# Weights cast by GpSimd's transfers, w_out centred and scaled in one operation, w in pairs of units, and a new order of work

**Chip, cores, metric.** One core of a Trainium2 chip. The metric is the device time of one execution in microseconds (us); every kernel was run several times on the chip that ran the kernel before in the same session. "Fast" and "slow" are states of an execution: slow is over 1.5% above the fastest of the same kernel.

## The reference

A linear attention (RWKV-6) over 4 sequences of 768 tokens with 8 heads of 48, then a feed-forward layer on 3072 tokens of width 384:

```python
state = w_t * state + k_t v_t^T                 # per head
y_t   = r_t (state + (u * k_t) v_t^T)
h     = y @ w_in                                # 384 x 1024
solu  = h * softmax(h)
out   = (solu - mean) / sqrt(var + 1e-6) * g_ln @ w_out     # 1024 x 384
```

All inputs are float32: r, k, v, w are 4 x 8 x 768 x 48 each, w_in and w_out 1.57 MB each.

## The kernel before

The tokens are cut into 24 units (six chunks of 128 tokens by four sequences). Each unit goes through some thirty stages, and a list of words, `ORDER`, fixes the order in which all engines get their work: `ldk3` loads k of unit 3, `lw3` takes the log of its w, `kp3` scales k and r of unit 3, `kt3` transposes them, `H0` is the first hidden product, `e0` and `he0` its exponential and product, `Oa0` its first output product. Each engine keeps that order, so a word that waits holds back every later word of its engine. A letter at the end of a word names the engine (a ScalarE, v VectorE, g GpSimd).

The inputs, in rows of 192 bytes, and both weights are asked for by SyncE, in one queue:

```python
sp.dma_start(out=L[name], in_=src[b, :, c * C:(c + 1) * C, :].rearrange("h t d -> t h d"))
...
def load_w_in(j):
    sp.dma_start(out=win_f[:, j, :], in_=win_v[:, j, :])
def load_w_out(half):
    part = slice(half * KF // 2, (half + 1) * KF // 2)
    sp.dma_start(out=wout_f[:, part, :], in_=wout_v[:, part, :])
```

w_in is cast on ScalarE (`win`). From w_out comes w2, whose rows are scaled by g_ln and centred: eight gains (`gw`), a mean product (`mean`), eight additions on GpSimd (`wt`):

```python
def setup_w_in(j, engine):
    copy(engine, win_sb[:, j, :], win_f[:, j, :])
def setup_gain(f, engine):
    ...
    engine.tensor_scalar(out=gw[:, f, :], in0=wout_f[:, f, :], scalar1=gr[:, f:f + 1], scalar2=None, op0=MULT)
def setup_mean():
    for f in range(KF):
        pe.matmul(m_ps, lhsT=mean_w, rhs=gw[:, f, :], start=(f == 0), stop=(f == KF - 1))
def setup_w2(f, engine):
    engine.tensor_add(out=w2[:, f, :DM], in0=gw[:, f, :], in1=mean_sb)
```

The start of the order, down to the first hidden products (weights are asked for at `ldwin` and `ldwout`):

```python
dm5 dm3 dm18 dm1 ldw0 ldr0 small dm16 dm8 ldk0 lw0 ldw1 ldr1 cum0 exp0 et0 lw1 rows cum1 ldk1 p0g ldw2 kp0 exp1 ubc kt0 p1g kr0v ldr2 M0 ldk2 ldv0 et1
kp1 lw2 m0a q0g kt1 kr1v ldwin2 cum2 q1g sel0 dg0 exp2 M1 dm10 et2 vb0a kp2 m1a ldwin1 ldv1 kt2 win2a dg1 dv0g kr2v win1a vb1a Y0 y0v sel1 ldwin0 M2
win0a dm6 X0 m2v dv1v ldwout0 dm4 p2g Y1 q2g S1 y1v ldwout1 qa2 gw1a gw0a dm2 X1 xT0v xT1v dg2 H0 H1 ldw3 e0 ...
```

The softmax here doesn't subtract the row's maximum and nothing guards it: scores larger than these inputs give would overflow.

Of the kernel before, what the change touches and what calls it, by code (L numbers as in the profile page):

```python
# [14 lines left out]
SQUARE = mybir.ActivationFunctionType.Square  # L15
IDENTITY = mybir.ActivationFunctionType.Identity
# [8 lines left out]
dm5 dm3 dm18 dm1 ldw0 ldr0 small dm16 dm8 ldk0 lw0 ldw1 ldr1 cum0 exp0 et0 lw1 rows cum1 ldk1 p0g ldw2 kp0 exp1 ubc kt0 p1g kr0v ldr2 M0 ldk2 ldv0 et1  # L25
kp1 lw2 m0a q0g kt1 kr1v ldwin2 cum2 q1g sel0 dg0 exp2 M1 dm10 et2 vb0a kp2 m1a ldwin1 ldv1 kt2 win2a dg1 dv0g kr2v win1a vb1a Y0 y0v sel1 ldwin0 M2
win0a dm6 X0 m2v dv1v ldwout0 dm4 p2g Y1 q2g S1 y1v ldwout1 qa2 gw1a gw0a dm2 X1 xT0v xT1v dg2 H0 H1 ldw3 e0 st1 S0 dm13 ldv2 gw4v gw6v gw3g he0 ldk3
gw5a dm12 dm17 ldw4 st0 gw7a ldr3 e1 ldk4 lw3 gw2g mean mean_sb:a vb2g ldw5 dv2g he1 Y2 ldr4 cum3 wt2g y2v exp3 lw4 et3 p3v hq0a wt3g cum4 wt1g X2 dm0
wt0g ldk5 dm9 ldr5 exp4 lw5 ldw6 wt4g kp3 S2 kt3 ldv3 cum5 st2 ldw7 wt7g ldv4 et4 kr3a xT2v wt6g ldr6 Oa0 kp4 p4v exp5 wt5g M3 q3v et5 m3a kt4 kr4v
ldk6 Oa1 kp5 hq1a H2 M4 q4g kt5 Ob0 ldv5 sel3 ldw8 lw6 vb3a e2 dg3 kr5a dv3g m4v sq0a dg4 vb4g dv4g p5g vb5g Ob1 ldr7 M5 lw7 ldk7 Y3x ldv6 he2 m5v qm0  # L30
q5g p6g y3a cum6 X3 xT3v sq1v Y4 qm1 exp6 y4v H3 lv0 lv1 et6 ldr8 X4 hq2v ldk8 kp6 Oa2 dg5 o0a xT4a dv5g p7g sto0 ldw9 S4 e3 S3 st4 st3 q6g H4 Y5 vb6g
q7g ldr9 o1a he3 kt6 lw8 S5 Ob2 e4 ldk9 y5v cum7 ldr10 he4 kr6a st5 X5 hq3a sq2a exp7 M6 Oa4 ldv7 ldk10 ldr11 Oa3 qm2 m6v cum8 ldv8 qa6 et7 xT5a sto1
dg6 ldr12 ldk11 lv2 kp7 qa7 Ob3 dv6g exp8 p8g ldw10 p9v kt7 et8 o2a dg7 sq3g kp8 H5 qm3 q8g hq4a lv3 ldv9 e5 ldw11 Y6x kr7v ldv10 p10g M7 vb7g o3v Ob4
ldw12 kt8 m7v y6a q10g lw9 X6 sq4v he5 cum9 xT6a qm4 ldk12 exp9 kr8a dg8 et9 dv7g Y7 hq5g H6 e6 sto2 kp9 Oa5 ldw13 kt9 y7v lv4 X7 dg10 q9g Ob5 kr9a
he6 vb8g ldv11 ldk13 dv8g ldr13 sq5a o4a M8 ldw14 hq6g m8v S7 M9 qm5 vb10g xT7a p11g ldv12 m9v lv5 Oa6 H7 dg9 st7 lw10 Y8 o5a e7 cum10 vb9g ldw15
exp10 Ob6 y8v he7 sq6g X8 sto3 et10 dv9g S6 kp10 ldk14 xT8a lw12 S8 q11g H8 lw11 lw13 cum11 st8 e8 dv10g st6 Oa7 qm6 kt10 Y9x p12g exp11 hq7v kr10a
lv6 Ob7 y9a he8 M10 et11 S9 ldw16 sto4 o6a ldr14 X9 xT9a kp11 cum12 qa11 Oa8 ldr15 exp12 hq8g m10v p13g ldv13 vb11g ldk15 st9 H9 sq7v et12 qm7 kt11
q12g ldv14 lw14 ldr16 kp12 ldk16 lv7 e9 Y10x q13g sto5 y10a o7v ldk17 kr11v he9 cum13 exp13 ldv15 et13 dg11 kt12 kp13 Ob8 X10 sto6 M11 kr12a sq8g Oa9
qa12 ldk18 dv11g ldr17 dg13 M12 m12v kt13 ldw17 vb12g xT10a qm8 S10 m11a sel11 H10 kr13v M13 lw15 st10 ldv16 hq9a Y11x lv8 p15g e10 y11a m13v vb13g
sto7 o8a Ob9 dg12 p14g ldr18 ldv17 sq9v dv12g p16g X11 ldw18 cum14 xT11a S11 he10 Y12 H11 exp14 S12 qm9 st11 y12v lv9 et14 kp14 q14g dv13g st12 hq10g  # L40
o9a ldv18 e11 Y13 X12 cum15 xT12a ldr19 he11 exp15 kt14 Oa10 y13v sto8 hq11g kr14a vb15a q15g lw16 S13 H12 vb14g et15 ldk19 kp15 e12 dg14 X13 M14 p17g
dv14g kt15 ldw19 m14v xT13a he12 kr15a Ob10 H13 q17g sto9 hq12g sq10a st13 M15 Y14 m15v ldv19 qm10 lv10 vb16g Oa11 e13 lw18 q16g S14 lw17 o10v y14v
cum16 he13 ldw20 exp16 dg15 et16 hq13v Ob11 dv15g X14 kp16 Oa12 p18g sq11a p19g xT14a st14 qm11 lv11 H14 Ob12 o11a e14 cum17 q19g kt16 sq12v ldk20 Y15
sto10 he14 exp17 q18g qm12 Oa13 sto11 kr16a et17 hq14g y15v cum18 kp17 lv12 Ob13 M16 ldr20 ldk21 o12v exp18 dg17 X15 vb17g sq13v kt17 m16a et18 qm13
Oa14 xT15v kp18 kr17v sel16 lv13 H15 o13a lw19 dg16 e15 kt18 M17 dv17g dv16g vb19g ldv20 kr18v m17a lw20 Ob14 Y16 he15 M18 y16v sq14v S16 qm14 dg18
cum19 X16 ldv21 hq15g xT16v m18a exp19 Oa15 H16 ldw21 sel17 S15 dg19 lv14 o14a et19 kp19 Y17 lw21 ldr21 st16 e16 cum20 sel18 vb18g st15 y17v exp20
Ob15 sto12 ldk22 ldr22 X17 sto13 kt19 sq15v ldv22 xT17a he16 dv18g Y18 qm15 kr19a dv19g kp20 p20v y18v hq16g H17 M19 Oa16 lv15 X18 q20g Ob16 m19v o15a
e17 xT18a ldw22 lw22 p22g cum21 sq16v he17 qm16 p21g dg20 ldw23 hq17g ldv23 exp21 Y19 kt20 H18 vb20g ldr23 Oa17 lv16 y19v kp21 q21g kr20v o16a cum22
e18 he18 dv20g kt21 exp22 Ob17 kr21a M20 X19 sq17g S17 qm17 m20a lv17 kp22 qa21 sel20 lw23 S18 xT19v sto14 o17a st17 hq18g M21 Oa18 ldk23 m21v kt22
cum23 H19 sto15 st18 exp23 kr22v vb21a kp23 dg21 dv21g sto16 Y20 Y21 vb22a M22 q22g S19 e19 m22a vb23g y20v X20 p23v st19 he19 q23g Ob18 kt23 xT20a  # L50
sq18v H20 qm18 kr23a sel22 M23 y21v lv18 o18a X21 dg22 hq19v xT21v Oa19 m23a dv22v dg23 sel23 Y22 Ob19 y22v e20 he20 H21 dv23g Y23 sto17 X22 sq19a
Oa20 y23v X23 qm19 lv19 hq20g o19a xT22v e21 xT23v H22 e22 he21 Ob20 sto18 hq21g sq20a qm20 lv20 H23 he22 Oa21 Oa22 sto19 Ob21 e23 hq22g sq21a o20v
qm21 lv21 Ob22 he23 hq23v Oa23 sto20 sq22v sq23a qm22 o21v Ob23 sto21 lv22 qm23 Oc23 o22v sto22 lv23 dm14 oz23v dm15 o23a stz23 dm7 sto23 dm11 dm19
# [25 lines left out]
def kernel(  # L79
# [14 lines left out]
    C = 128  # L94
# [23 lines left out]
    def load(name, src):  # L118
        def stage(i):
            c, b = units[i]  # L120
            L = live[i]
            if name in "kr":

                if "k_and_r" not in L:
                    L["k_and_r"] = io.tile([C, 2, H, 64], F32, tag="kr_in", name="kr_in")
                t = L["k_and_r"][:, "kr".index(name)]
            else:
                t = io.tile([C, H, 64], F32, tag=name + "_in", name=name + "_in")
            L[name] = t[:, :, :D]
            sp.dma_start(out=L[name], in_=src[b, :, c * C:(c + 1) * C, :].rearrange("h t d -> t h d"))  # L130
        return stage
# [4 lines left out]
    win_f = consts.tile([128, KM, DF], F32)  # L136
    win_v = moe_w_in.rearrange("(ko ki) f -> ki ko f", ki=128)
    wout_f = consts.tile([128, KF, DM], F32)
# [6 lines left out]
    def load_w_in(j):  # L145
        sp.dma_start(out=win_f[:, j, :], in_=win_v[:, j, :])

    def load_w_out(half):
        part = slice(half * KF // 2, (half + 1) * KF // 2)
        sp.dma_start(out=wout_f[:, part, :], in_=wout_v[:, part, :])  # L150
# [3 lines left out]
    nc.gpsimd.memset(uti_neg, -1.0)  # L154
    nc.gpsimd.affine_select(out=uti_neg, in_=uti_neg, compare_op=ALU.is_ge, fill=0.0, base=0,
                            pattern=[[1, C]], channel_multiplier=-1)
    uts = consts.tile([C, C], BF16)
    nc.gpsimd.memset(uts, 1.0)
    nc.gpsimd.affine_select(out=uts, in_=uts, compare_op=ALU.is_gt, fill=0.0, base=0,
                            pattern=[[1, C]], channel_multiplier=-1)  # L160
    ident = consts.tile([C, C], BF16)
    make_identity(nc, ident)
# [12 lines left out]
    lw_t = [consts.tile([C, H, 64], BF16, name=f"lw{j}") for j in range(NR)]  # L175
    kp_t = [consts.tile([C, 2, H, 64], BF16, name=f"kp{j}") for j in range(NR)]
    for j in range(NR):
        nc.vector.memset(lw_t[j][:, :, D:], 0.0)
        nc.vector.memset(kp_t[j][:, :, :, D:], 0.0)
# [7 lines left out]
    mean_w = consts.tile([128, 128], BF16)  # L187
    nc.vector.memset(mean_w, -1.0 / DF)
    nc.vector.memset(w2[:, :, DM:], 1.0 / RDF)

    ident_f = consts.tile([KF, KF], F32)
    make_identity(nc, ident_f)
# [4 lines left out]
    gw = consts.tile([128, KF, DM], BF16)  # L197
# [12 lines left out]

    def copy(engine, out, in_):
# [10 lines left out]
    def setup_w_in(j, engine):  # L222
        copy(engine, win_sb[:, j, :], win_f[:, j, :])


    def setup_gain(f, engine):
        if engine is act:
            act.activation(out=gw[:, f, :], in_=wout_f[:, f, :], func=COPY, scale=gr[:, f:f + 1])
        else:
            engine.tensor_scalar(out=gw[:, f, :], in0=wout_f[:, f, :], scalar1=gr[:, f:f + 1], scalar2=None, op0=MULT)  # L230

    def setup_mean():
        m_ps = small.tile([128, DM], F32, tag="s", name="mean_ps")
        for f in range(KF):
            pe.matmul(m_ps, lhsT=mean_w, rhs=gw[:, f, :], start=(f == 0), stop=(f == KF - 1))
        live[0]["mean_ps"] = m_ps

    def setup_mean_copy(engine):
        copy(engine, mean_sb, live[0]["mean_ps"])

    def setup_w2(f, engine):
        engine.tensor_add(out=w2[:, f, :DM], in0=gw[:, f, :], in1=mean_sb)


    def log_w(i):
        L = live[i]
        L["lw"] = lw_t[i % NR]
# [392 lines left out]
```

## Time and profile before

| | first profile (the prediction's) | second look, taken after it |
|---|---|---|
| time of that execution | 156.91 us, slow | 151.97 us (a single execution, so its state is not decided) |
| span | 155.2 us | 150.3 us |
| first hidden product starts | 20.06 us | 20.06 us |
| matmuls from 25 to 30 us | 34 | 45 |
| matmuls from 80 to 120 us | 628 | 694 |

The median was 151.41 us (151.08 to 151.83).

### The profile page before, as it was taken

The numbers are of one execution on the slowest core, as the hardware profiler recorded it, in microseconds if no ns is written. First come the engines' busy times: TensorE is split into PE (matmuls) and PEld (weight loads), VectorE is DVE, ScalarE is ACT, GpSimd is POOL, SyncE is SP. The second block draws the span as 40 slices with busy tenths as digits, with TensorE's granted clock in tenths as the row PEclk, the third lists the DMA queues.
The fourth block names the chain that finished last, engine by engine and source line by source line (L and its number), as shares of the span: only waits on it lengthen the run. The fifth ranks groups of instructions, "written<-read, shape, count | busy, mean of one in ns | idle before, by whom it ended". The sixth has DMA issues, their size and how long they took to land.

```text
span 155.2 us, 5295 instructions
## 1 busy us (share of the span) xinstructions
PE 140.4 (90%) x2156; PEld 109.7 (71%) x2156; DVE 129.4 (83%) x231; ACT 120.2 (77%) x232; POOL 123.1 (79%) x152
## 2 busy tenths in 40 slices
PE   6877897699999899999999799939999999999993
PEld 2344584477786787888788587737888778889771
DVE  7546738899998898999976989999889999998661
ACT  4456767989898979798989698829899888895742
POOL 3375965997999799999947999977799899976800
PEclk9999999999999999999999999999999999999999
DMA  4999997989999999899796999999989311011013
GB/s 95 201 185 301 380 303 152 213 160 190 208 202 184 204 229 187 194 205 233 154 205 157 218 217 200 228 250 180 215 196 211 100 51 55 2 55 55 18 62 127
DMA packets 104970, 27.09 MB, mean 175 GB/s; under 512 B 100329, under 2 KB 104562, under 8 KB 104946
## 3 DMA queue, kind: packets, MB, share of 16 engines
q1 hardware_dynamic: 104946, 26.75, 76.4%
q8 instruction: 17, 0.28, 0.7%
q14 instruction: 7, 0.06, 0.1%
HBM read 22.03 MB, written 4.72 MB: 172 GB/s over the span
## 4 chain that ended last, share of the span: by engine, by line
PE 50%; DMA 14%; DVE 10%; SPq 8%; POOL 8%; ACT 4%; issue 3%; POOLq 0%; DVEq 0%
PE o_ps L71 18%; PE h_ps L71 13%; SPq L71 8%; DMA kr_in<-in_k_dram 8%; DMA wout_f<-in_moe_w_out_dram 6%; POOL w L71 5%; PE kr_ps L71 5%; PE cum_ps L71 3%; PE m_ps L71 3%; PE y_ps L71 3%; PE s_ps L71 3%; DVE hq L71 3%; DVE kp L71 2%; PE x_ps L71 2%; DVE he L71 1%
## 5 line engine op out<-in xcount | busy, mean ns | idle before, releaser
L71 PE MATMUL o_ps<-w,he 128*128 128x385 bf16 (+2 forms) x200 | 42.2, 315 | 0.3 <-ACT sq L71 0.3
L71 PE MATMUL h_ps<-xT,win_sb 128*128 128x128 bf16 x576 | 36.0, 219 | 0.1
L71 PEld LDWEIGHTS <-win_sb 128*128 128x128 bf16 x576 | 32.9, 98 | 0.9 <-issue 0.2
L71 PE MATMUL o_ps<-inv_col,e 128*128 128x1 bf16 x192 | 31.1, 165 | 0.0
L71 DVE TENSOR_TENSOR he<-h_ps,e 128x1024 bf16<-128x1024 f32 x24 | 29.2, 1217 | 2.2 <-ACT e L71 2.2
L71 POOL TENSOR_TENSOR hq<-he 128x1024 bf16<-128x1024 bf16 x14 | 26.5, 1895 | 3.7 <-DVE he L71 2.4
L71 ACT ACTIVATE e<-h_ps 128x1024 bf16<-128x1024 f32 x24 | 24.5, 1021 | 6.2 <-PE h_ps L71 6.1
L71 PEld LDWEIGHTS <-he 128*128 128x128 bf16 x208 | 19.7, 96 | 10.5 <-issue 0.3
L71 ACT ACTIVATE cum_ps<-cum_ps 128x772 f32<-128x772 f32 (+1 forms) x24 | 19.2, 801 | 8.8 <-PE cum_ps L71 7.6
L71 DVE TENSOR_TENSOR kp<-cum_ps,kr_in 128x768 bf16<-128x768 f32 x24 | 22.7, 948 | 0.6 <-DMA kr_in<-in_r_dram 0.5
L71 POOL TENSOR_TENSOR q<-p,u_bc 128x384 bf16<-128x384 bf16 x23 | 22.0, 962 | 0.6 <-DVE p L71 0.5
L71 POOL TENSOR_TENSOR p<-kr_in 128x384 bf16<-128x384 f32 x18 | 17.9, 1001 | 5.4 <-DMA kr_in<-in_k_dram 5.4
L71 PEld LDWEIGHTS <-kp 128*128 128x128 bf16 x272 | 17.6, 102 | 4.4 <-DVE kp L71 2.3
L71 POOL TENSOR_TENSOR dv<-vb,dg 128x384 bf16<-128x384 bf16 x22 | 18.2, 830 | 2.3 <-ACT vb L71 1.5
L71 DVE TENSOR_TENSOR m<-m_ps,uts 128x1024 bf16<-128x1024 f32 x14 | 17.0, 1223 | 3.1 <-PE m_ps L71 3.0
L71 PEld LDWEIGHTS <-e 128*128 128x128 bf16 x192 | 18.3, 96 | 0.1
L71 PE MATMUL kr_ps<-ident,kp 128*128 128x128 bf16 x192 | 15.9, 230 | 1.4 <-DVE kp L71 1.4
L71 PEld LDWEIGHTS <-kr 64*128 64x128 bf16 (+1 forms) x272 | 10.7, 98 | 4.9 <-DVE kr L71 2.2
L71 ACT ACTIVATE lw<-w_in 128x384 bf16<-128x384 f32 x23 | 11.7, 523 | 2.7 <-DMA w_in<-in_w_dram 2.7
L71 ACT COPY kr<-kr_ps 128x1024 bf16<-128x1024 bf16 x13 | 13.2, 1014 | 0.5 <-PE kr_ps L71 0.4
L71 POOL TENSOR_SCALAR_AFFINE_SELECT m<-m 128x1024 bf16<-128x1024 bf16 x10 | 11.0, 1103 | 2.5 <-ACT m L71 2.4
L71 PE MATMUL cum_ps<-lw,uti_neg 128*128 128x384 bf16 x24 | 8.3, 347 | 4.8 <-DVE kp L71 3.3
(93 smaller groups left out, 284.3 us busy)
## 6 DMA issues: line engine op xcount, KB each, us to landing
w_in<-in_w_dram SPq DMA_DIRECT2D x24, 192.0 KB, 4.2
kr_in<-in_r_dram SPq DMA_DIRECT2D x24, 192.0 KB, 3.8
kr_in<-in_k_dram SPq DMA_DIRECT2D x24, 192.0 KB, 3.8
v_in<-in_v_dram SPq DMA_DIRECT2D x24, 192.0 KB, 3.8
out_dram<-o SPq DMA_DIRECT2D x23, 192.0 KB, 3.1
win_f<-in_moe_w_in_dram SPq DMA_DIRECT2D x3, 512.0 KB, 6.1
wout_f<-in_moe_w_out_dram SPq DMA_DIRECT2D x2, 768.0 KB, 8.8
out_dram<-o SPq DMA_DIRECT2D x2, 96.0 KB, 1.6
```

Source lines behind the costliest of these rows:

```text
L71: made = make(*args, **kwargs)
```

## The change

Intent: take the casts of w_in off ScalarE and the gains off three engines, by letting GpSimd's transfers cast; form w2 for five of eight blocks in one VectorE operation; log w for two units at once. GpSimd makes its masks first and then asks for half of w_out and two thirds of w_in before anything else. The order of all the work is new too.

```diff
     def load_w_in(j):
-        sp.dma_start(out=win_f[:, j, :], in_=win_v[:, j, :])
+        pool.dma_start(out=win_sb[:, j, :], in_=win_v[:, j, :])          # to bf16
     def load_w_out(half):
-        sp.dma_start(out=wout_f[:, part, :], in_=wout_v[:, part, :])
+        pool.dma_start(out=wout_f[:, part, :], in_=wout_v[:, part, :])   # to float32r
-    def setup_w_in(j, engine): ...
+    def setup_gain_wide(engine):
+        copy(engine, g_wide, gr.unsqueeze(2).to_broadcast([128, KF, 128]))
     def setup_mean(half):
-            pe.matmul(m_ps, lhsT=mean_w, rhs=gw[:, f, :], ...)
+            pe.matmul(live[0]["mean_ps"], lhsT=g_wide[:, f, :], rhs=wout_f[:, f, :], ...)
     def setup_w2(f, engine):
-        engine.tensor_add(out=w2[:, f, :DM], in0=gw[:, f, :], in1=mean_sb)
+        if "scaled" in live[f]:      # three blocks: gain on ScalarE, addition on GpSimd
+            engine.tensor_add(out=w2[:, f, :DM], in0=w2[:, f, :DM], in1=mean_sb)
+        else:                        # five blocks: one operation on VectorE
+            engine.scalar_tensor_tensor(out=w2[:, f, :DM], in0=wout_f[:, f, :].bitcast(F32), scalar=gr[:, f:f + 1], in1=mean_sb,
+                                        op0=MULT, op1=ALU.add)
     ...                              # w: one transfer and one log for units i, i + 1, from unit 4 on
 ORDER (start)
+ldw0 iwout0 dm1 dm12 dm10 iwin2 lw0 dm16 dm18 ldr0 dm2 cum0 exp0 iwin1 small ldk0 et0 kp0 ldw1 rows kt0 ubc kr0v lw1 cum1 ldr1 ldk1 ldw2 exp1 lw2 et1
+ldr2 p0g kp1 ldk2 M0 kt1 cum2 iwin0 m0a exp2 dm6 dm14 ldv0 ldr3 p1v kr1v ldw3 ldv1 q0g iwout1 vb0a sel0 M1 ldk3 m1a q1g dg0 et2 kp2 kt2 lw3 ...
```

## The prediction

> **What bounds the kernel now.** I read the page's busy shares first, then its forty slices, then the windows that count TensorE's matmuls by stage, and last the chain of work and the timeline where that count is poor.
>
> Busy shares:
>
> ```profile
> PE 140.4 (90%) x2156; PEld 109.7 (71%) x2156; DVE 129.4 (83%) x231; ACT 120.2 (77%) x232; POOL 123.1 (79%) x152
> ```
>
> Four engines lie within 20 us of each other, so no single one is a bound with room behind it. The slices show the stages:
>
> ```profile
> PE   6877897699999899999999799939999999999993
> POOL 3375965997999799999947999977799899976800
> DMA  4999997989999999899796999999989311011013
> GB/s 95 201 185 301 380 303 152 213 160 190 208 202 184 204 229 187 194 205 233 154 205 157 218 217 200 228 250 180 215 196 211 100 51 55 2 55 55 18 62 127
> ```
>
> The transfers are busy nine tenths of the time to about 118 us, then nearly idle: 33 us of work remain after the last input. From about 40 us TensorE is full. The windows say how full, since each gives the number of matmuls in brackets:
>
> ```profile
> 20.00:25.00 5.00, 5.00 (x65) 3.97 (x63) 2.11 (x6) 3.17 (x7) 2.47 (x2) 1.00 0.81 211
> 25.00:30.00 5.00, 2.75 (x34) 1.77 (x33) 4.79 (x8) 4.63 (x8) 4.58 (x6) 1.00 1.09 216
> 30.00:40.00 10.00, 9.37 (x151) 7.24 (x150) 9.35 (x15) 8.58 (x15) 9.17 (x11) 1.00 0.93 183
> 60.00:80.00 20.00, 20.00 (x339) 16.33 (x338) 18.08 (x29) 18.09 (x40) 18.74 (x28) 1.00 0.97 200
> 100.00:120.00 20.00, 17.29 (x305) 14.30 (x305) 18.82 (x32) 15.76 (x31) 16.87 (x17) 1.00 0.96 213
> ```
>
> (The columns after the stretch are its length, then PE, weight loads, DVE, ACT and POOL, the granted clock, the DMA share and GB/s.) The undisturbed rate is 339 matmuls in 20 us, 17 per us; 2156 of them would take 127 us. The span is 155.2, so 28 us are lost. By stage, length minus count over 17: 13.8 in the first 20 us (105 matmuls), 1.2 from 20 to 25, 3.0 from 25 to 30, 1.1 from 30 to 40, 1.4 from 40 to 100, 2.1 from 100 to 120, 0.2 to 140, 3.7 after it (26.5 in all; a matmul across a border counts twice). Two thirds are lost before 30 us, which is where this change works. The chain of waits crosses the same stretch:
>
> ```profile
> 13.97 9.87 DMA wout_f<-in_moe_w_out_dram
> 23.87 1.12 ACT gw L71 x2
> 24.99 0.81 ACT e L71
> 25.80 0.51 ACT lw L71
> 26.31 0.38 ACT mean_sb L71
> 26.69 0.07 issue
> 26.75 7.75 POOL w L71 x8
> ```
>
> The second half of w_out lands at 23.87; VectorE had stood idle 2.6 us for it and ScalarE 1.8 us. Both had work behind it: the log of unit 3's w was only done at 26.3, and TensorE waited. Then GpSimd spends 7.75 us on the eight additions that give w2.
>
> The profiled execution was long (155.2 us against a median of 151.41), so I use the profile for differences only and apply them to 151.41.
>
> **What the Trainium skill says.** "DMA: Bandwidth & Descriptors", section "SWDGE vs HWDGE vs iDMA", says that a casting transfer can only be issued from GpSimd, whose cores write the descriptors in software, and that a float32r destination counts as a cast. The kernel before issues everything from SyncE, so its trace cannot show that cost. The same page, "Issuing engines are not separate DMA queues", says that all issuers share the same 16 engines. The slices agree as far as one issuer can: the rate rises to 380 GB/s while weights move, against about 200 with the 192-byte rows of the inputs, and the share stays near nine tenths in both. "SBUF — State Buffer", "Who interferes with whom", says that GpSimd shares ports with VectorE, and that a VectorE operation with two SBUF inputs contends with GpSimd's reads. The trace fits: VectorE's square of he takes 1464 ns and GpSimd's 1895 ns on the same 128x1024 bf16. "FP8 and Floating Point Precision", "TensorE Precision Notes", has float32 at four passes and a reduced form that truncates four-byte data. The trace has only true float32 (922 ns each for two matmuls of 384 columns, u_ps) and bf16 (325 ns, mean_ps); the new product should lie between.
>
> **The change part by part.**
>
> *w_in.* Three casts of 1046 ns leave ScalarE: 3.1 us, at 15.7 to 20.0 us. The last one ends just as the first hidden product starts (20.06), so it was on the start's path by about 1 us.
>
> *w_out.* Removed: six gains (ScalarE 4 x 607 ns, GpSimd 2 x 1249, VectorE 2 x 418; eight in all) and eight GpSimd additions, 7.75 us. Put in: three ScalarE gains (1.8), three GpSimd additions (3 x 1.0), five fused VectorE operations. A two-input operation with a float32 SBUF side takes 997 ns (p) and a bf16 one 544 (dv), so I take 0.55 to 1.0 each, 2.8 to 5 us. GpSimd is relieved by 4.8 + 2.5 us and VectorE gets about 3 more. TensorE's mean no longer waits for the gains, but for a widened gain (one ScalarE copy of 128x1024, some 1.05 us) and the landing. The eight products go from 1.67 us together to an estimated 3, halfway to the float32 rate: 1.3 us lost.
>
> *w in pairs.* Units 0 to 3 stay single; the other twenty need ten transfers and ten logs instead of twenty. From 511 ns (384) and 1046 ns (1024) of the float32 casts, a column costs 0.84 ns, so a log of 768 takes 0.84 us against 2 x 0.523: 0.2 saved ten times, 2.0 us of ScalarE. Rows remain 192 bytes, so the transfer time does not change.
>
> *The order.* The whole order of work is new, and moves more than the operations. By counts: squares of he GpSimd 14 to 10, VectorE 5 to 9; masks on GpSimd 10 to 13; kr copies ScalarE 13 to 10. Summed with the durations of the groups, ScalarE loses about 4 us, GpSimd about 10, VectorE gains about 5 (129 to 134). TensorE has the same matmuls but for two.
>
> *The start.* GpSimd now makes all masks first and then queues half of w_out and two thirds of w_in, so these start at about 3 to 4 us beside the first inputs, where before they waited behind eleven of them. Ahead of the first hidden product TensorE now has unit 3's cumulated sums and transposes too, so 14 input loads (2.75 MB) and all weights (3.15 MB) are needed: 5.9 MB. The kernel before has moved 1465 x 3.88 = 5.7 MB by 23.3 us and 5.9 by some 24.5; as the transfers were busy from 4 us, the new one can hardly be earlier. I put the first hidden product at 24 to 26 us, against 20.06. By then 127 matmuls are done (warm-ups included), where the kernel before had about 170, 2.5 us ahead. In return all later work is ready: no weight is still to land, so I take away the 3.0 us lost from 25 to 30 and most of the 1.1 after it. Balance of the start: 4.1 - 2.5 = +1.6, less 1.3 for the mean, about zero to +1.
>
> *The rest.* From 40 us on only 7.4 us are lost, 3.7 of them in the end, which has the same form. With GpSimd 10 us lighter some waits like those between 80 and 120 (3 us lost) should go; I take 1 us. Sum: 1.4 us faster, 151.4 to 150.0. The pairing, and the casts as such, are mostly beside other work.
>
> **The rivals.** (1) *The weights hold up the first inputs.* Big weight packets alternate with 192-byte ones, unit 0's k and r land some 3 us late, and everything after follows. For it: the transfers are already full from 4 us. Against: nothing but the sum of bytes decides when unit 3 is ready. It would make 152 to 154. (2) *VectorE becomes the bound.* It had 18.8 and 19.5 of 20 us from 100 to 140, and gets 5 us more. Against: 3 of these lie before 40 us, and less GpSimd work means less port contention. It would make 151 to 153. (3) *The order is simply better.* The start loses nothing (the first hidden product at 21) and GpSimd's relief removes the stalls: 3 + 1 + 3 us, 145 to 147. For it: w_out's lateness is what idled two engines at 21 to 24. Against: the count of bytes. (4) *GpSimd's transfers are issued late*, because descriptor writing waits for VectorE or for p of unit 0, which stands in the queue before the last third of w_in. The late third would then hold the first hidden product to 28 us: 153 to 155.
>
> **Range and chances.** 150.0 us is the sum. Rival 3 is as likely as the others together, so the range is 146.3 to 153.6. Faster by over 2% means below 148.4: 0.31. Within 2%: 0.57. Slower (above 154.4): 0.12.
>
> **What would show it.** Right: the weights landed by 18 us, the first hidden product between 24 and 26 us, no wait for w_out on ScalarE or VectorE, over 75 matmuls from 25 to 30 us where 34 stood, GpSimd near 113 us busy, VectorE near 134, the mean's eight products near 3 us. Wrong: a first hidden product at 21 us or before (rival 3), at 28 or later with TensorE waiting for kr_in (1) or win_sb (4), windows after 60 us in which VectorE is full and TensorE under 16 matmuls per us (2), or an end that is lost outside the first 40 us, which I count as nearly unchanged.

## The result, and the profile after

| | median (range) | executions |
|---|---|---|
| changed kernel | 158.90 us (158.13 to 159.22) | 4 |
| kernel before, same session | 151.26 us (151.08 to 151.83) | 4 |

The ratio is 1.049, 95% interval 1.044 to 1.054: slower. (Ratios are the mean time of one kernel's fast runs over that of the other's of the same rounds, so not quite the ratio of the medians quoted.)

Where the time goes is read first from the count of matmuls by stage. The windows view of the kernel before; the columns are those that the prediction explains:

```profile
0.00:10.00 10.00, 7.06 (x29) 3.18 (x29) 5.70 (x36) 4.45 (x6) 4.09 (x15) 1.00 0.84 166
10.00:20.00 10.00, 7.99 (x75) 5.17 (x76) 7.39 (x13) 6.56 (x9) 7.33 (x10) 1.00 1.05 341
20.00:25.00 5.00, 5.00 (x69) 4.13 (x68) 3.06 (x8) 4.10 (x7) 3.28 (x4) 1.00 0.90 197
25.00:30.00 5.00, 3.25 (x45) 2.35 (x44) 4.95 (x10) 4.46 (x8) 4.66 (x6) 1.00 1.11 218
30.00:40.00 10.00, 9.14 (x153) 7.26 (x152) 9.81 (x16) 8.46 (x17) 9.92 (x13) 1.00 1.04 205
```

The same windows of the changed kernel:

```profile
0.00:10.00 10.00, 5.18 (x15) 2.06 (x15) 4.35 (x31) 2.60 (x3) 4.81 (x17) 1.00 0.89 187
10.00:20.00 10.00, 4.63 (x38) 3.07 (x38) 3.84 (x8) 2.90 (x5) 2.47 (x5) 1.00 1.18 249
20.00:25.00 5.00, 4.36 (x43) 2.60 (x42) 2.65 (x5) 3.10 (x5) 4.46 (x6) 1.00 1.12 218
25.00:30.00 5.00, 4.83 (x60) 3.50 (x57) 4.04 (x7) 4.00 (x6) 3.09 (x4) 1.00 0.90 180
30.00:40.00 10.00, 8.45 (x117) 6.71 (x113) 8.89 (x14) 8.65 (x12) 8.25 (x9) 1.00 0.98 195
```

By 40 us the kernel before has done 371 matmuls and the changed one 273. The 98 missing, at the full rate of 17 per us, are 5.8 us; the spans differ by 6.6. From 40 to 120 us the two count 1362 and 1352, and the granted clock is 1.00 in both. So it is lost in the start, in two stretches: 173 against 96 matmuls in the first 25 us, and 153 against 117 from 30 to 40. Between them, from 25 to 30, the changed kernel is ahead, as hoped.

Both stretches show on VectorE. Its timeline in the kernel before (start, length, operation; in brackets the idle time before it and what ended that):

```profile
5.98 0.95 DVE L71 TENSOR_TENSOR kp<-cum_ps,kr_in 128x768 bf16<-128x768 f32 x1
...
9.97 0.95 DVE L71 TENSOR_TENSOR kp<-cum_ps,kr_in 128x768 bf16<-128x768 f32 x1
...
27.97 0.94 DVE L71 TENSOR_TENSOR kp<-cum_ps,kr_in 128x768 bf16<-128x768 f32 x1
...
29.76 0.96 DVE L71 TENSOR_TENSOR kp<-cum_ps,kr_in 128x768 bf16<-128x768 f32 x1
...
36.46 1.21 DVE L71 TENSOR_TENSOR he<-h_ps,e 128x1024 bf16<-128x1024 f32 x1
```

and in the changed kernel:

```profile
9.00 0.96 DVE L72 TENSOR_TENSOR kp<-cum_ps,kr_in 128x768 bf16<-128x768 f32 x1 [2.94 <-DMA kr_in<-in_k_dram]
...
14.73 0.95 DVE L72 TENSOR_TENSOR kp<-cum_ps,kr_in 128x768 bf16<-128x768 f32 x1
...
35.53 4.07 DVE L72 SCALAR_TENSOR_TENSOR w<-wout_f,gr,mean_sb 128x384 bf16<-128x384 f32 x4
...
39.59 0.94 DVE L72 TENSOR_TENSOR kp<-cum_ps,kr_in 128x768 bf16<-128x768 f32 x1
...
42.05 1.21 DVE L72 TENSOR_TENSOR he<-h_ps,e 128x1024 bf16<-128x1024 f32 x1
```

The first `kp` waits for k of unit 0 and comes 3.0 us later, the second 4.8 us later. Then, at 35.5 us, four of the fused operations stand in a row, 4.07 us, ahead of the next `kp` (unit 4), which the kernel before had done at 29.8. The third unit's `he` comes at 42.05 instead of 36.46.

The changed kernel's chain of work that ended last (start, length, what) says what the first wait was:

```profile
4.82 4.20 SPq L72
...
9.06 9.21 DMA w_in<-in_w_dram
18.29 0.53 ACT lw L72
...
28.88 2.69 PE h_ps L72 x48
```

SyncE is stuck for 4.2 us in asking for k of unit 1, where the kernel before needs 0.76, and w of unit 2, asked for at 9.06, is used at 18.29. The same log in the kernel before (ScalarE's timeline):

```profile
9.31 0.52 ACT L71 ACTIVATE lw<-w_in 128x384 bf16<-128x384 f32 x1
```

From this log to the first hidden product it is 10.4 us in the changed kernel (28.7) and 10.8 in the kernel before (20.06), so the 9 us by which w of unit 2 is late are handed on almost whole. The weights themselves had all landed by 18.3 us. The transfers as a whole were not slower: counting w_in as it is read (float32), both kernels have moved about 8.65 MB by 37.6 us. What differs is the order of arrival.

### The profile page after: what moved, and what is told of

Read it like the earlier page. It is cut to its first block, busy times and chain, and to the rows that moved or that the text cites. A ratio compares the mean times of both kernels' runs of the same rounds, so it can differ in the third digit from the quotient of the medians.

```text
span 156.9 us, 5267 instructions
## 1 busy us (share of the span) xinstructions
PE 139.1 (89%) x2154; PEld 109.4 (70%) x2154; DVE 128.8 (82%) x232; ACT 117.8 (75%) x223; POOL 119.0 (76%) x148
## 4 chain that ended last, share of the span: by engine, by line
PE 71%; DMA 8%; DVE 7%; SPq 5%; ACT 5%; issue 1%; POOL 0%; ACTq 0%
PE o_ps L72 24%; PE h_ps L72 19%; PE kr_ps L72 6%; DMA w_in<-in_w_dram 6%; PE cum_ps L72 6%; SPq L72 5%; PE y_ps L72 5%; PE m_ps L72 4%; PE s_ps L72 3%; PE x_ps L72 3%; DMA kr_in<-in_r_dram 2%; DVE m L72 2%; DVE kp L72 1%; DVE w L72 1%; DVE he L72 1%
## 5 line engine op out<-in xcount | busy, mean ns | idle before, releaser
L72 ACT ACTIVATE e<-h_ps 128x1024 bf16<-128x1024 f32 x24 | 24.5, 1022 | 6.6 <-PE h_ps L72 6.4
L72 PEld LDWEIGHTS <-he 128*128 128x128 bf16 x208 | 19.6, 96 | 10.4
L72 POOL TENSOR_TENSOR p<-kr_in 128x384 bf16<-128x384 f32 x20 | 20.3, 1022 | 4.3 <-DMA kr_in<-in_k_dram 4.3
L72 POOL TENSOR_TENSOR dv<-vb,dg 128x384 bf16<-128x384 bf16 x24 | 20.9, 874 | 3.2 <-DMA kr_in<-in_k_dram 2.1
L72 POOL TENSOR_TENSOR hq<-he 128x1024 bf16<-128x1024 bf16 x10 | 18.9, 1894 | 4.1 <-DVE he L72 4.1
L72 POOL TENSOR_SCALAR_AFFINE_SELECT m<-m 128x1024 bf16<-128x1024 bf16 x13 | 14.7, 1130 | 9.2 <-ACT m L72 8.2
L72 PEld LDWEIGHTS <-e 128*128 128x128 bf16 x192 | 18.3, 96 | 1.0 <-issue 0.8
L72 ACT ACTIVATE lw<-w_in 128x768 bf16<-128x768 f32 (+1 forms) x13 | 10.0, 769 | 10.3 <-DMA w_in<-in_w_dram 10.3
L72 DVE TENSOR_TENSOR m<-m_ps,uts 128x1024 bf16<-128x1024 f32 x11 | 13.4, 1218 | 1.1 <-PE m_ps L72 1.0
L72 ACT CAST m<-m_ps 128x1024 bf16<-128x1024 f32 x13 | 13.1, 1006 | 0.8 <-PE m_ps L72 0.7
L72 DVE COPY kr<-kr_ps 128x1024 bf16<-128x1024 bf16 x14 | 9.5, 687 | 4.0 <-PE kr_ps L72 3.8
```

Source lines behind the costliest of these rows:

```text
L72: made = make(*args, **kwargs)
```

## The experiments

Two theories stood at the start. **A, arrival:** weights that move ahead of the inputs displace the ones that the order needs next. **B, order:** the new order is worse in itself, since unit 3's sums and transposes stand ahead of the first hidden product. A third question was what the fused operation is worth. The expectations name more theories: **C**, casting transfers cost in themselves; **D**, a second queue takes the transfers from whatever inputs are due; **E**, the operations are the loss, above all the fused one. **F** is used twice: in run 7 for the sum of bytes, in run 10 for the place of unit 3 in the order.

The granted clock is not the same in all runs. In the profiles of both kernels and of runs 2, 8, 13 and 14 it is 1.00 in every stretch to 40 us. In those of runs 3, 6, 7, 9, 10, 11, 12, 15 and 18 it is 0.50 to 0.58 from 10 to 20 us, and in those of runs 3, 4, 5, 6, 11, 16, 17 and 18 it is 0.55 to 0.86 from 30 to 40. How much of their loss goes with this, these runs do not separate. The kernel before hardly shows it: its fast executions beside the experiments took 150.6 to 152.0 us at a mean clock of 0.999 to 1.00, and 150.9 to 152.7 at 0.954 to 0.966. Where an execution near the full clock bears on a reading, it is named.

**1. A second look at the kernel before** (no edit).

> The kernel before, once more, for a profile of an ordinary (fast) execution: the first profile was of an execution of 156.9 us where the median is 151.3. Both theories need it as a base. I expect about 151 us, a span near 149.5, the same first 40 us (the first hidden product near 20, about 350 matmuls by 40 us), and fewer than 100 + 17 us of lost matmuls between 80 and 120.

151.97 us, span 150.3, 694 matmuls from 80 to 120 us. The stalls late in the first profile belonged to that execution.

**2. The weights later in the new kernel, in two bursts.**

```diff
-ldw0 iwout0 dm1 dm12 dm10 iwin2 lw0 ... exp0 iwin1 small ... cum2 iwin0 m0a ... q0g iwout1 vb0a sel0 M1
+ldw0 dm1 dm12 dm10 lw0 ... exp0 small ... cum2 m0a ... q0g iwin2 iwin1 iwin0 vb0a sel0 iwout0 iwout1 M1
```

> The changed kernel with its five weight transfers, still GpSimd's and still casting, moved behind the first p and q of GpSimd's queue (w_in) and behind the first mask (w_out). Theory A (weights issued at 3 to 5 us alternate with the inputs of units 0 to 2 and hold them up): k of unit 0 lands near 6 us instead of 9, w of unit 1 near 7 instead of 12.3, matmuls in the first 20 us rise from 53 to 80 or more, and the time falls by 4 to 7 us, to 152 to 155. Theory B (the new order is what costs, whoever moves the weights): within 1.5 us of the changed kernel, 157 to 160. Theory C (casting transfers cost more wherever they are): the same as B, and the weights take over 7 us each to land.

159.14 us, ratio 1.053: no gain, as B and C expected. The first stretch was repaired (37 matmuls to 10 us instead of 15), but the burst hit the next inputs. SyncE's timeline:

```profile
8.52 0.81 SPq L72 DMA_DIRECT2D v_in<-in_v_dram  x1
...
10.13 5.79 SPq L72 DMA_DIRECT2D w_in<-in_w_dram  x1
15.96 4.31 SPq L72 DMA_DIRECT2D v_in<-in_v_dram  x1
```

v of unit 0, asked for at 8.52, was used only at 19.80, and SyncE stood 10 us in two requests. A in its simple form (late is enough) failed here.

**3. New code in the old order**, weights in two bursts from GpSimd.

```diff
 ORDER of the kernel before, with
-ldwin2 ldwin1 ldwin0 ldwout0 ldwout1   win2a win1a win0a   gw0..7   wt0..7g
+q1g iwin2 iwin1 iwin0    sel0 iwout0 iwout1    gm:a gw1a gw0a gw5a    wt2v wt3v wt4v wt6v wt7v wt0g wt1g wt5g
```

> All the operations of the change (casting transfers, fused w_out, pairs of w) in the order of the kernel before; the weight transfers stand in GpSimd's queue behind its first four products and masks, so at about the time at which SyncE issued them. Theory A: no early weights, so near the kernel before, 149 to 153 us. Theory B: the order is the old one, so also 149 to 153. Theory C, or a costly fused operation on VectorE (1196 ns each in the changed kernel): 154 or more.

157.81 us, ratio 1.042, where A and B both expected 149 to 153, although the first hidden product was at 19.94 us. ScalarE's timeline shows the loss after it:

```profile
23.45 1.12 ACT L72 ACTIVATE w<-wout_f,gr 128x384 bf16<-128x384 f32 x2 [7.86 <-DMA wout_f<-in_moe_w_out_dram]
```

In ScalarE's order the gain stands ahead of the exponential of unit 0, so that waits too. The old order does not rescue the new code. That fits C's number, but the wait is for a transfer that was asked for late, not for a cast shown to be slow.

**4. Old code in the new order**, all weights plain on SyncE's queue, both halves of w_out ahead of k of unit 3.

```diff
 ORDER of the changed kernel, with
-iwout0 iwin2 iwin1 iwin0 iwout1   gm:a meanA   (pairs of w)
+ldk2 ldwin2   ldv0 ldwin1   ldv1 ldwin0   ldwout0 ldwout1 ldk3   win2a win1a win0a   gw0..7   mean   wt0..7g
```

> The operations of the kernel before in the new order, with the weights issued by SyncE where the kernel before has them (behind the inputs of units 0 to 2). Theory A: no early weights, so most of the loss goes: 150 to 154 us. Theory B: the new order keeps the loss: 156 to 160 us. First hidden product: by 23 us in A, after 26 us in B.

165.53 us, ratio 1.094, the worst of all and outside both forecasts. There is no second queue and no cast in this kernel, and still its chain has

```profile
17.13 8.79 DMA kr_in<-in_k_dram
```

k of unit 3 lands at 25.9 behind w_out. So a second queue is not needed for the harm; weights ahead of what the order needs next are enough. In addition, its eight gains and eight additions stand where the new order has no room for them; how the loss divides between the two, no run separates.

**5. The kernel before, weights plain, but asked for by GpSimd at about 11 to 15 us.**

```diff
-        sp.dma_start(out=win_f[:, j, :], ...)      # and wout_f
+        pool.dma_start(out=win_f[:, j, :], ...)    # and wout_f
-... ldwin2 ... ldwin1 ... ldwin0 ... ldwout0 ... ldwout1
+... q1g ldwin2 ldwin1 ldwin0 sel0 ldwout0 ldwout1
```

> The kernel before, all operations and its order kept, but its five weight transfers (plain float32, no cast) are issued from GpSimd's queue behind its first two q (w_in) and first mask (w_out), so at about 11 to 15 us, where SyncE issued them at 9 to 14. Theory D (a second queue: its large packets are served beside the input queue and take the transfer engines from whatever inputs are due, wherever in time): slower than before by 3 to 7 us, 154 to 158, and one input issued beside the weights takes over 7 us to land. Theory C (it is the cast): no slower than before, 150 to 152.5. Theory E (the loss is in the operations, above all the fused w_out on VectorE): the same, 150 to 152.5.

153.56 us, ratio 1.014 (1.010 to 1.018): 2.1 us for asking on a second queue, at nearly the same time, between the numbers of D and of C and E. Two of the executions had a clock of 1.00 and took 153.3 and 153.4, so the 2 us are not the clock's.

**6. The same at the changed kernel's early places** (half of w_out and two thirds of w_in first of all).

```diff
-... q1g ldwin2 ldwin1 ldwin0 sel0 ldwout0 ldwout1
+ldwout0 ldwin2 ldwin1 dm5 ... p0g ldwin0 ... q0g ldwout1
```

> The kernel before with its five plain weight transfers issued from GpSimd's queue where the changed kernel issues them: half of w_out and two thirds of w_in behind the masks at about 3 us, the rest behind the first p and the first q. Theory A (early weights hold up the first inputs): k of unit 0 lands near 9 us instead of 6, w of unit 1 at 12, and the time rises by 3 us or more above the kernel before and above the same transfers issued at 11 us (153.6): 154.5 to 158. If only the burst counts and not where it falls: 153 to 154.

160.17 us; three of the four executions count as slow (one of them with a mean clock of 0.999), so no ratio is given. The one fast execution took 156.19, against 153.32 to 154.51 for run 5: at least 1.7 us more. The profile, of a slow execution at a mean clock of 0.925, has the changed kernel's signature at the very start. VectorE:

```profile
11.02 0.96 DVE L72 TENSOR_TENSOR kp<-cum_ps,kr_in 128x768 bf16<-128x768 f32 x1 [5.00 <-DMA kr_in<-in_k_dram]
```

The kernel before had this at 5.98. Old code, old order, no cast: an early burst alone delays the first input by 5 us. This is a wait for a transfer, so a lower clock of TensorE is not its cause; that it is worth 5 us in a fast execution too, no profile shows.

**7. The changed kernel with its weights asked for one at a time.**

```diff
-ldw0 iwout0 ... iwin2 ... iwin1 ... iwin0 ... iwout1
+... q0g iwin2 ... sel0 iwin1 ... q1g iwin0 ... dv0g iwout0 ... dv1g iwout1
```

> The changed kernel, its weight transfers not in a burst but one at a time in GpSimd's queue: behind the first q, the first mask, the second q, and the first two dv. Theory D: inputs get the transfer engines between the weights, so v of unit 0 lands before 15 us and the time falls by 2 to 5 us, to 154 to 157. If the sum of bytes ahead of the first hidden product is what counts (theory F: the new order needs 5.9 MB there), no change, 157.5 to 160.

155.55 us, ratio 1.028: 3.4 us better than the changed kernel (measured in another session), with nothing changed but the places of five requests, and at a lower clock (0.938 to 0.945). The first hidden product came at 26.15. 4.1 us were still lost.

**8. The fusion undone** (all eight gains on ScalarE, all eight additions on GpSimd).

```diff
-gw1a gw0a gw5a                wt0g wt1g wt5g wt3v wt2v wt6v wt4v wt7v
+gw0a .. gw7a                  wt0g wt1g wt5g wt3g wt2g wt6g wt4g wt7g
```

> The changed kernel with w_out's fusion undone: all eight gains on ScalarE, all eight additions on GpSimd, VectorE does none of it. In the changed kernel VectorE spends 35.5 to 39.6 us in four fused operations of about 1.0 us and the sums of the next unit's keys wait behind them. Theory E: faster than the changed kernel by 1.5 to 4 us, 155 to 157.5. Theory D or F: within 1 us of it, 158 to 160, since GpSimd then has 8 us in the same place.

163.75 us, ratio 1.082: 4.9 us slower than with it. In the new order the fusion is worth having.

**9. w singly.**

```diff
-                if i >= 4:
+                if False:
-        both = range(i, i + 2) if i >= 4 else range(i, i + 1)
+        both = range(i, i + 1)
```

> The changed kernel with w loaded and logged one unit at a time again (twenty transfers and twenty logs instead of ten and ten, each second one directly behind the first). No theory makes the pairs matter: ScalarE 2 us busier but not the bound. Within 1 us of the changed kernel, 158 to 160. If the pairs cost (units wait for a load of twice the size), faster by 1 us or more.

158.55 us against 158.90, the ranges overlapping: the pairing does not matter.

**10. Spread weights, and unit 0's hidden product ahead of unit 3.**

```diff
-y0v exp3 S0 dv1g X0 ... xT0a ... H0 ... e0 he0
+y0v X0 xT0a H0 e0 he0 S0 cum3 exp3 dv1g ...
```

> The changed kernel with its weights spread as before, and unit 0's transposed output, its copy, first hidden product, exponential and product moved ahead of unit 3's cumulated sum and of unit 1's output: in the spread run w_in had landed by about 19 us but the first hidden product started at 26.2, behind unit 3's transposes, whose k landed at 23. Theory F (what is left of the loss is that the new order puts unit 3 ahead): first hidden product at 19 to 21, time down by 1.5 to 4 us from 155.6, to 151.5 to 154. If what is left lies in the stage of w2 and later, no change: 155 to 156.5.

158.46 us, ratio 1.049, worse than run 7. The product came at 19.98, but its `he` only at 23.79 with VectorE idle for 7.4 us, and unit 3 came later in turn. An execution at a clock of 0.997 took 158.65, so the clock is not the reason. The edit does not bear B out, though it moved words blindly: it does not prove that no such order is good.

**11. New code, old order, weights one at a time.**

```diff
-q1g iwin2 iwin1 iwin0    sel0 iwout0 iwout1
+q0g iwin2   q1g iwin1   sel0 iwin0   dv0g iwout0   p2g iwout1
```

> All operations of the change in the order of the kernel before (157.8 with the weights in two bursts), the weights spread: one behind each of GpSimd's first q, second q, first mask, first dv and third p. Theory D: the second half of w_out and the inputs of unit 3 and 4 no longer collide, 3 us or more faster than 157.8: 152 to 155. If the additions on VectorE are what costs in this order, less than 1.5 us: 156.5 to 158.

157.80 us, ratio 1.040, the same as run 3; ScalarE again waited 8.0 us for w_out, to 23.3. Spreading is no remedy where w_out is needed by 20 us.

**12. The kernel before, only w_in cast by transfers.**

```diff
-        sp.dma_start(out=win_f[:, j, :], in_=win_v[:, j, :])
+        pool.dma_start(out=win_sb[:, j, :], in_=win_v[:, j, :])
-ldwin2 ldwin1 ldwin0 win2a win1a win0a
+p1g ldwin2   q1g ldwin1   sel0 ldwin0
```

> One part alone: the kernel before with only w_in cast by three GpSimd transfers, one at a time behind its second p, second q and first mask (about 10, 11.5 and 13 us); w_out stays with SyncE and its engines. It takes three casts of 1.05 us from ScalarE, the last of which ended at 20.0 as the first hidden product started. By my account of the change: first hidden product at 18.5 to 20 and 0.5 to 1.5 us faster, 149.5 to 151. Theory D: the three weights still take turns with the inputs, so no gain, 151 to 153. Theory C (casting transfers cost in themselves): over 153.

153.42 us, ratio 1.0075 (0.9996 to 1.0153): no gain shown from the three casts that ScalarE is spared. The one execution at a clock of 1.00 took 151.72, the same as the kernel before in that session (151.69); the others, one of them slow and the one profiled, had 0.954 to 0.955. In that profile the first hidden product comes at 22.2 us, after TensorE was idle 2.6 us for w_in.

**13 and 14. No weight traffic at all**, in both kernels. The weights are replaced by constants made on the core; the results are wrong.

```diff
-... ldwin2 ldwin1 ldwin0 ldwout0 ldwout1        (iwin, iwout in the changed kernel)
+    nc.vector.memset(win_f, 0.05)               # win_sb in the changed kernel
+    for a in range(2):
+        act.copy(out=wout_f[:, 4 * a:4 * a + 4, :]..., in_=own[:, 0, 0:1].to_broadcast([128, 4 * DM]))
```

> The kernel before with no weight transfers at all: win_f and wout_f are filled on the core with constants ahead of the first input (VectorE and ScalarE, both idle then), so the result is wrong on purpose; all operations and their order stay. 3.1 MB less have to move before the start. Theory A (traffic decides): about 148 us, as the 3 us of waits for w_out at 21 to 26 us go. It is mostly the measure for free_after: what counts is the difference of the two.

> The changed kernel with no weight transfers, filled in the same way, wrong on purpose; its operations and their order stay, and GpSimd no longer issues transfers. Theory A (the weights' second queue displaces the inputs, and nothing else is wrong): within 1 us of free_before or below it, since fewer operations are left on ScalarE and GpSimd; a gain of some 10 us on the changed kernel. Theory B (the new order of work is worse at the start): still 4 us or more above free_before, with the first hidden product over 4 us later.

153.07 and 153.43 us, ratios 1.0133 (1.0094 to 1.0173) and 1.0142 (1.0106 to 1.0177) to the kernel before: equal. This tells A from B: without weights to move, the new order and the new operations lose nothing against the old ones. Neither do they gain. Both runs missed their level, as the kernel before became slower without its weights. VectorE's timeline of that run shows why:

```profile
4.65 2.62 DVE L186 MEMSET win_f<- 128x3072 f32 x1 [0.59 <-issue]
...
11.71 0.94 DVE L71 TENSOR_TENSOR kp<-cum_ps,kr_in 128x768 bf16<-128x768 f32 x1
```

The constants were not free: the fill lies on the path, and the second `kp` comes at 11.71 instead of 9.97. My estimate of its cost is that difference, 1.7 us. Taking it off, an estimate, the weights' traffic costs the kernel before about 0.1 us (153.07 - 1.7 against 151.25), and the changed kernel about 7.2 (158.9 against 153.43 - 1.7). The second is nearly all of the 7.6 us lost. It contains both ways in which traffic hurts, inputs displaced and weights late.

The same two runs put the stretch from 30 to 40 us right. The windows of the kernel before and of the changed kernel, both without weight traffic:

```profile
30.00:40.00 10.00, 9.46 (x148) 7.07 (x145) 9.82 (x16) 8.65 (x17) 9.92 (x12) 1.00 0.49 97
30.00:40.00 10.00, 7.97 (x122) 5.98 (x121) 9.88 (x13) 7.38 (x13) 7.83 (x9) 1.00 0.94 186
```

The four fused operations stand in a row here too, 4.07 us from 29.04, and the new order does 26 matmuls less in this stretch (36 less with the weights). Without the traffic it can afford that, as it is 40 ahead by 30 us (243 against 203). With the traffic it is 62 behind by then (156 against 218). So nearly all that the traffic takes, it takes in the first 30 us; the row of fused operations is a price of the new order that its lead was to pay for.

**15. Spread weights with w_in back on SyncE's queue** and its casts back on ScalarE; w_out from GpSimd as in run 7.

```diff
-q0g iwin2 ... sel0 iwin1 ... q1g iwin0
+ldk2 iwin2 ... ldv0 iwin1 ... ldv1 iwin0 ... m1a win2a ... vb1a win1a ... xT0a win0a
```

> spread_weights, but w_in plain on SyncE's queue at the kernel before's places (behind k of unit 2, v of unit 0, v of unit 1) with its three casts back on ScalarE; w_out stays a casting transfer from GpSimd, late. Theory A: below 153.5, as only w_out is left on the second queue, and late. Theory B: 155 to 157, no better than spread_weights (155.6), as the order is the same and ScalarE has 3 us more to do.

156.84 us, ratio 1.037 (155.76 in the execution nearest the full clock, 0.998): A's number was wrong and B's right, although run 14 speaks against B. The chain says why:

```profile
16.56 8.35 DMA kr_in<-in_k_dram
```

k of unit 3 was in flight from 16.6 to 24.9 us, while GpSimd's w_out requests (at 15.99 and 19.53) moved beside it. In the old order that would delay a later unit; in the new one unit 3's transposes stand ahead of the first hidden product, which came at 26.8. The order sets which input counts, the traffic makes it late: A and B are not rivals here but two halves.

**16. The other half: the old order with only w_out by casting transfers,** fused, and w in pairs; w_in as in the kernel before.

```diff
-ldwout0 ldwout1   gw0..7   wt0..7g
+sel0 iwout0   dv0g iwout1   gm:a gw1a gw0a gw5a   wt2v wt3v wt4v wt6v wt7v wt0g wt1g wt5g
```

> The other half of it: the kernel before's order, with w_in plain on SyncE's queue and cast on ScalarE as before, and w_out by casting transfers from GpSimd behind two early operations (masks of unit 0 and 1), centred and scaled in one operation, w in pairs. Theory A: w_out displaces the inputs of units 1 and 2, some 152.5 to 154. If w_out early were right after all, its landing by 20 us would end the wait for it at 21 to 24 us, and the run would be below 150. Theory B has the kernel before's order here, so it expects 151 or less.

154.75 us, ratio 1.024, just above A's 152.5 to 154. The first hidden product was at 19.9, so units 0 to 2 were not held up, and the second half of w_out landed at 23.6, about as late as in the kernel before. The loss is from 30 to 40 us: 122 matmuls against 153. Run 18 has the same form without any of these transfers.

**17. Run 15 with w_out asked for behind unit 3's inputs.**

```diff
-dv0g iwout0 ... dv1g iwout1
+p3g iwout0 iwout1
```

> fifo_w_in with one move: both halves of w_out are asked for behind p of unit 3 on GpSimd, which itself waits for k and r of unit 3, so they can no longer hold those up. If the second queue's displacement of the inputs is the cost (theory A, with the new order making unit 3 the input that counts): k of unit 3 lands at 19 to 20 us instead of 24.9, the first hidden product is at 21 to 23 instead of 26.8, and the time 152 to 154.5; w_out then lands near 28 us and takes some of it back. If the new order is bad by itself (theory B): no better than 156.

156.41 us, ratio 1.033. The mechanism came out as A had it, the time did not: k of unit 3 landed at 20.6 instead of 24.9 and the first hidden product came at 23.6 instead of 26.8, but the gain was handed on. The chain:

```profile
16.18 4.42 DMA kr_in<-in_k_dram
...
22.54 7.80 DMA wout_f<-in_moe_w_out_dram
...
30.39 1.65 PE mean_ps L72 x4
```

w_out now lands at 30.35, and in TensorE's order its mean stands ahead of the next hidden product. The transfers can bring unit 3 or w_out in time, and the new order asks for both.

**18. The kernel before, four of the eight additions on VectorE.**

```diff
-wt3g ... wt1g ... wt4g ... wt6g
+wt3v ... wt1v ... wt4v ... wt6v
```

> The kernel before, with four of the eight additions that give w2 (1, 3, 4, 6) on VectorE instead of GpSimd, where the eight stand as one block of 7.75 us. If the block is what empties TensorE at 25 to 30 us, 149 to 150; if the inputs of units 3 and 4 are (k and r used only at 29.8 us in the kernel before), within 1% of it, 150.5 to 152. Measures what could be had from unloading GpSimd without touching the transfers.

154.69 us, ratio 1.024 (1.021 to 1.027): a loss where I had thought of a gain. VectorE's timeline:

```profile
27.94 2.31 DVE L71 TENSOR_TENSOR w<-gw,mean_sb 128x384 bf16<-128x384 bf16 x3
30.18 0.94 DVE L71 TENSOR_TENSOR kp<-cum_ps,kr_in 128x768 bf16<-128x768 f32 x1
...
39.37 1.21 DVE L71 TENSOR_TENSOR he<-h_ps,e 128x1024 bf16<-128x1024 f32 x1
```

Three additions stand ahead of `kp`: 30.18 instead of 27.97, and unit 2's `he` is 2.9 us later than in the kernel before, close to the 3.2 us lost. In this stretch VectorE is the full engine (9.81 of 10 us from 30 to 40 in the kernel before), and GpSimd's block of 7.75 us lay beside it. The four additions take 2.7 us of VectorE, and the 3.2 us lost are no less than that.

No version beat the kernel before.

## Why the prediction was wrong

The forecast was 150.0 us in a range to 153.6; it came out at 158.9. By its own steps:

- **The step that failed is the dismissal of its first rival:** "Against: nothing but the sum of bytes decides when unit 3 is ready." The sum of bytes was right (8.65 MB by 37.6 us in both kernels), and the 5.9 MB that the prediction asked for had been moved by 23.5 us (an estimate from the GB/s of the slices), before the 24.5 that it reckoned. But the sum decides only where everything summed is wanted at the same time. The 3 MB of weights went ahead of inputs wanted sooner, and some 10 us of work still follow the use of w of unit 2. k of unit 0 was used at 9.00 instead of 5.98, w of unit 1 at 12.3 instead of 6.5, and the first hidden product came at 28.7, not at 24 to 26. Runs 6 and 7 show the early request at work, runs 13 and 14 that the traffic is worth nearly the whole loss. The rival's mechanism was right, and its sign (a product at 28 us or later, with waits for inputs) came; its size ("some 3 us late", 152 to 154) was too small, as the wait returned for w of units 1 and 2. What the two queues do to each other packet by packet, no run shows. The Trainium skill, "DMA: Bandwidth & Descriptors", "Queues, rings and completion order", has each transfer engine take turns between the queues packet by packet. The late k in run 6 fits that; but in run 4 a k was in flight for 8.8 us with one queue.
- **"In return all later work is ready"** failed too. I took away 4.1 us for the stretch from 25 to 40. From 25 to 30 there were 60 matmuls (I wanted over 75; 45 stood before), and from 30 to 40 there were 117 against 153. The stretch was never limited by w_out's landing alone: VectorE is busy 9.8 of its 10 us in the kernel before and 8.9 in the changed one. Five fused operations took 5.3 us together, against 2.8 to 5 estimated, four of them in one row ahead of unit 4's `kp`. The estimate missed what GpSimd does beside them. The first of the row starts before GpSimd's additions and takes 0.61 us; the three beside those additions and the fifth, beside GpSimd's products, take 1.18 to 1.27. In run 16, with GpSimd idle:

```profile
31.41 0.60 DVE L72 SCALAR_TENSOR_TENSOR w<-wout_f,gr,mean_sb 128x384 bf16<-128x384 f32 x1
```

  So the work on w2 that was meant to run side by side was slowed by being so; GpSimd's three additions took 3.5 us where 3 were reckoned. The rival "VectorE becomes the bound" was dismissed because "3 of these lie before 40 us"; just those cost, though run 14 shows that the lead at 30 us would have covered it. Run 18 shows the price of such work in the old order. In the new order the alternative is dearer still (run 8).
- **The microsecond after 40 us** rested on stalls of a slow execution (run 1). It did not come: 1352 matmuls against 1362 from 40 to 120 us. The 1464 ns that the prediction gives for VectorE's square, as a sign of contention with GpSimd, is from the same execution: a mean of five, of which one took 4.09 us and the median 0.69.
- **Right:** the weights had landed by about 18 us; w_out made neither ScalarE nor VectorE wait in the changed kernel; the pairing is worth nothing measurable; ScalarE was busy 117.8 us (about 116 follows from the forecast). That the casts of w_in lie beside other work fits run 12, but their place was taken there by a wait for w_in, so it is not shown.
- **Sizes that were off:** the mean's products cost 1.9 us instead of 3. VectorE came to 128.8 us, not 134, and GpSimd to 119.0, not 113.

What stays open: whether some order exists in which the casting transfers pay. For the orders tried, run 14 bounds it: even with no weights to move, the new code and order were no faster than the old. What the cast alone costs also stays open, as no run moves the same weights at the same places with and without it; so does the part of the lower clock in the runs that had it.

## What to carry to other kernels

Where the transfers are busy from the start, moving a transfer earlier means moving another later: ask which input the program's order needs next, not when all bytes will be there. An operation is cheap or dear by what stands behind it on its engine, so before work is moved off an engine, look which engine is full in that stretch. And look at the state of the profiled execution before a late stall is counted as something to win.

## What the Trainium skill lacked or had wrong

- "DMA: Bandwidth & Descriptors", "Rules for kernel authors": the advice to issue a transfer early and wait late lacks its condition. With a DMA share of 0.89 and 1.18 in the first two stretches of 10 us, the early request of the weights cost; the same five requests spread out took 155.6 us instead of 158.9.
- The same page, "Issuing engines are not separate DMA queues", says that a second issuer saves only issue time. That section does not say that it changes which transfer lands first, and how much that costs (the turns that the page describes under "Queues, rings and completion order" give no size): the same plain weights from a second queue cost 2.1 us at 11 to 15 us, and asked for first of all they made the first `kp` 5.0 us later.
- The same page gives no figure for a casting transfer. Here the median landing of a third of w_in took 6.8 us with the cast (changed kernel) and 6.3 plain from GpSimd (run 5), of half of w_out 6.6 and 9.2. These were asked for at different times, so they do not give the cost of the cast, and none stands out.
- "FP8 and Floating Point Precision", "TensorE Precision Notes", gives no speed for the reduced float32 form: a product of 384 columns took a median of 340 ns against 326 in bf16, its weight load 189 ns against 97, and all eight products 1.92 us against 1.46.
